# Attention and max-of-three kernel: ScalarE's background casts behind the copies of transposes, transposes ahead of the products where a group begins, and a tile order that alternates by heads

## The chip, the core and the metric

One NeuronCore of a Trainium2 chip runs the whole program. The metric is the device time of one execution in microseconds (us). A kernel's time is the median of its runs. The profile is of one execution, taken apart by engine: TensorE (PE, with its weight loads as PEld), VectorE (DVE), ScalarE (ACT), GpSimd (POOL), and SyncE (SP), whose queue issues almost all DMAs.

## What is computed

Attention with a relative-position bias that a small network makes, for 4 batches, 8 heads, 576 positions and 64 channels a head, and behind it a feed-forward stage with the greatest of three products:

```python
scores = scale * np.matmul(q, k.transpose(0, 1, 3, 2))
h = np.maximum(x @ w1 + b1, 0.0)          # x: relative log distances, 576 x 576
bias = h @ w2                             # 576 x 576 x 8 heads
scores = scores + bias.transpose(2, 0, 1)[None, :, :, :]
scores = scores - np.max(scores, axis=-1, keepdims=True)
attn = np.exp(scores)
attn = attn / (np.sum(attn, axis=-1, keepdims=True) + 1e-09)
out = np.matmul(attn, v)
...
x = out.transpose(0, 2, 1, 3).reshape(B * S, H * D)      # 2304 x 512
h = np.maximum(np.maximum(x @ w1, x @ w2), x @ w3)       # 2304 x 768
return h @ w_out                                         # 2304 x 512
```

## The kernel before

The program has three stages. The first (to about 60 us) makes the bias for all heads and writes it to DRAM (`bias_d`). The second is attention, to about 334 us. The third is the feed-forward stage (`moe`), to the end; it multiplies in blocks, with every fp32 operand as a sum of a high and a low part.

Attention runs over *units*. A unit is a pair of heads (`hp`, 4 of them) of one batch (`b`, 4 of them): 16 units, taken in 8 *pairs* of units, two pairs per head pair. The 576 query rows of a unit are four tiles of 128 rows and 64 left over; the two leftovers of a pair of units share a fifth tile, the mixed one (`MIX`). A pair of units therefore has nine tiles, in the order of `STEPS` (L180): four of the first unit (0, 1, 2, 3), the mixed one, four of the second unit (2, 3, 0, 1). 72 tiles make 72 steps; five more empty the pipeline (`LAG` = 5).

Step n (`step`, L367) does the following, engine by engine, in program order:

- `front` (L237): TensorE multiplies queries by keys for tile n, in three terms of high and low parts, into two PSUM tiles `s` (one a head).
- then products (`pv`, L347) that stand in the list `pvq`: exponentials by values. A *group* is the products of one unit for 256 query columns (group 0) or 320 (group 1, with the leftover); it has five pieces (`NTQ + 1`), four over key tiles `vt` and one over the leftover keys `vl`. One to three pieces run in a step, by the list in L381, so that a group begins in the steps n with n modulo 9 equal to 1, 3, 5 and 7 and ends in the step behind it.
- `shift` (L260) on VectorE: adds the bias tile `bias_t[t]` (names `bias_75` to `bias_79` for the tiles t = 0 to 4), scales, and finds the row's extreme. `expo` (L272) on ScalarE: the exponential `e` with its row sum `sm`, for both heads.
- `split_x` (L361) on VectorE: copies a group's results from PSUM to `xb`.
- background (`more`, L391): the generators `w0`, `ex` and `lx` convert the weights of the last stage and split x. Each `next` issues one instruction on ScalarE, VectorE or POOL.
- `load_bias` (L168): in the second half of a head pair's last pair, the bias tile just used is loaded anew for the next head pair, by SP's queue.
- `norm` (L284): 1/sum on VectorE, multiplied on POOL, for step n − 1.
- `prep` (L212): ScalarE casts k or q of a later unit to its high part (`kh`, `qh`, L220) and POOL subtracts for the low part (`kl`, `ql`, L223).
- `flip` (L299) for tile n − 5: TensorE transposes the normalized exponentials, eight blocks into two PSUM tiles `tp` (L316; two buffers, one a head) and one block `lp` for leftover keys (L320). ScalarE copies head 0's `tp` and `lp` to the tile `et` (L411), VectorE head 1's (L413). For the mixed tile each of these copies is two, one for each unit. `et` is what the products read.

Every engine takes its instructions in the order in which this code issues them. Line 409 to 413 of `step`, before:

```python
tp0, tp1, left = self.flip(f)
for x in tp0 + left:
    nc.scalar.copy(*x)
for x in tp1:
    nc.vector.tensor_copy(*x)
```

Of the kernel before, what the change touches and what calls it, by code (L numbers as in the profile page):

```python
# [19 lines left out]
def kernel(  # L20
# [12 lines left out]
    nc = tc.nc  # L33
# [146 lines left out]
    STEPS = [(0, 0), (0, 1), (0, 2), (0, 3), (2, NTQ), (1, 2), (1, 3), (1, 0), (1, 1)]  # L180
# [7 lines left out]
    GW = 128 * 2  # L188

    class Attention:  # L190
# [46 lines left out]
        def front(self, n):  # L237
            pair, y = fronts[n]
            which, t = STEPS[y]
# [20 lines left out]
        def shift(self, n, h):  # L260
            t = STEPS[fronts[n][1]][1]
# [37 lines left out]
        def flip(self, n):  # L299
            pair, y = sched[n]  # L300
            which, t = STEPS[y]
# [27 lines left out]
        def queue_pv(self, un, c0, w0, ea, el):  # L329
            hp, b = units[un]  # L330
            u = self.data[un]
            made = []

            def pair(c):
                def run():
                    if c == 0:
                        self.split_x()

                        if un == len(units) - 1 and not c0:
                            made.append(ps_s("pvlast")[:, 0, 0:w0])  # L340
                        else:
                            made.append(psums[-1].tile([128, w0], F32, tag="pv", bufs=1, name=f"pv{un}_{c0}"))
# [5 lines left out]
                    if c == NTQ:  # L348
                        col = (b % (B // 2)) * S + c0
                        slot = ((1, 0), (2, 3))[hp // 2][b // (B // 2)]  # L350
                        for x in range(NX):
                            lo, hi = max(col, TW * x), min(col + w0, TW * x + TW)
                            if lo < hi:
                                self.done.append((pv[:, lo - col:hi - col],
                                                  raws[x][slot][:, hp % 2, lo - TW * x:hi - TW * x]))
# [11 lines left out]
        def step(self, n, more=()):  # L367
            m, f = n - 1, n - LAG
            if n < NSTEP:
                pair, y = fronts[n]  # L370
                which, t = STEPS[y]
# [18 lines left out]
            last = None  # L390
            for w in more:  # L391
                if last != "scalar":
                    last = next(w, None)
            if n < NSTEP and units[2 * pair + 1][1] == border[-1] and which and units[2 * pair][0] + 1 < HP:
                load_bias(units[2 * pair][0] + 1, t)
            if 0 <= m < NSTEP:
                self.norm(m)
            if n < NSTEP:
                k = n - (NS * pair + 6)
# [8 lines left out]
            if back:  # L408
                tp0, tp1, left = self.flip(f)
                for x in tp0 + left:  # L410
                    nc.scalar.copy(*x)  # L411
                for x in tp1:
                    nc.vector.tensor_copy(*x)  # L413
                pair, y = sched[f]
                for at, un, g in ((1, 0, 0), (MIX, 0, 1), (6, 1, 1), (8, 1, 0)):
                    if y == at:
# [579 lines left out]
```

## Time and profile before

| what | value |
|---|---|
| median of 3 runs | 613.27 us |
| lowest, highest | 609.05, 617.02 us |
| the profiled execution | 615.38 us |
| its span on the core | 613.6 us |
| TensorE busy | 584.1 us, 95% |
| VectorE, ScalarE, POOL busy | 438.4, 341.5, 318.1 us |
| mean granted clock of TensorE in the profiled execution | 0.989 of full |

The span runs from the first to the last instruction that the profile shows; the execution's own time is 1.8 us longer. A busy share is of the whole span, over stages with different limits. Matmuls are pipelined, their ends in the profile are modelled, and durations of neighbours overlap; how long a block of matmuls holds TensorE is read from its start to the start of the next block. In a row of the timeline, the bracket gives the engine's idle time before the instruction and what ended it.

### The profile page before, as it was taken

The page shows a single profiled execution, that of the slowest core. Times are in us where ns is not written, and L with a number is a line of the kernel's source. Part 1 is how long each engine was busy: PE and PEld are TensorE (multiplying, and loading weights), DVE is VectorE, ACT ScalarE, POOL GpSimd, SP SyncE. Part 2 cuts the span into 40 slices and gives each one's busy share as a digit, 9 for nine tenths or more (in the row PEclk, how much of TensorE's full clock was granted, in tenths as well). Part 3 has the DMA queues.
Part 4 walks back from the last instruction along what each step waited for, and adds up shares of the span by engine and source line. Part 5 has one row for each costly group of instructions (what it writes and reads, how often), then busy time and mean ns, then how long its engine had stood idle before and what let it go on. Part 6 is the DMA issues. An engine that isn't in the chain of part 4 may idle for free.

```text
span 613.6 us, 12110 instructions
## 1 busy us (share of the span) xinstructions
PE 584.1 (95%) x4368; PEld 467.0 (76%) x4368; DVE 438.4 (71%) x907; ACT 341.5 (56%) x790; POOL 318.1 (52%) x312
## 2 busy tenths in 40 slices
PE   8999999999979989898999999999999999999997
PEld 4456656566656757566666999999999999988886
DVE  7995688587777868677865889997999756722211
ACT  7996877777786878578764662223132122332332
POOL 2775655648465565538462025668766874600000
PEclk9999999899999999799999999999999999999999
DMA  5998418440764429241000042242114211754541
GB/s 168 263 360 275 133 42 286 131 140 36 219 211 121 129 79 282 79 136 46 21 21 35 1 138 68 88 138 69 35 36 137 87 35 35 228 164 150 170 146 70
DMA packets 70380, 76.84 MB, mean 125 GB/s; under 512 B 22832, under 2 KB 50864, under 8 KB 70320
## 3 DMA queue, kind: packets, MB, share of 16 engines
q1 hardware_dynamic: 70176, 75.77, 39.4%
q8 instruction: 35, 0.57, 0.4%
q10 hardware_dynamic: 144, 0.29, 0.1%
q14 instruction: 25, 0.20, 0.1%
HBM read 49.69 MB, written 26.36 MB: 124 GB/s over the span
## 4 chain that ended last, share of the span: by engine, by line
PE 78%; ACT 10%; DVE 4%; issue 4%; DMA 3%; POOL 0%; ACTq 0%; DVEq 0%; SPq 0%
PE pv L347 12%; PE p L530 10%; PE p L529 10%; PE p L531 10%; PE tp L316 8%; PE s L256 7%; ACT e L278 5%; PE o L802 4%; PE o L805 4%; PE o L803 4%; PE bp L135 3%; PE s L249 2%; DMA bias<-bias_d 1%; PE c L529 1%; PE c L531 1%
## 5 line engine op out<-in xcount | busy, mean ns | idle before, releaser
L290 POOL TENSOR_SCALAR e<-e,rc 128x576 f32<-128x576 f32 x144 | 105.6, 746 | 103.0 <-DVE rc L287 63.9
L278 ACT ACTIVATE e<-sn,nm 128x576 f32<-128x576 f32 x144 | 110.7, 771 | 61.5 <-DVE nm L266 58.8
L266 DVE CUSTOM_DVE_ANT_0 sn<-s,bias 128x576 f32<-128x576 f32 x144 | 103.3, 755 | 33.3 <-PE s L256 19.4
L347 PE MATMUL pv<-et,vt 128*64 128x320 f32 (+1 forms) x496 | 81.5, 441 | 16.0 <-ACT et L411 15.8
L316 PEld LDWEIGHTS tp<-ident,e 128*128 128x128 f32 x576 | 62.1, 141 | 32.6 <-issue 25.0
L413 DVE COPY et<-tp 128x512 f32<-128x512 f32 (+1 forms) x80 | 49.7, 630 | 42.7 <-PE tp L316 42.7
L316 PE MATMUL tp<-ident,e 128*128 128x128 f32 x576 | 79.4, 281 | 0.3 <-DVE et L413 0.2
L347 PEld LDWEIGHTS pv<-et,vt 128*64 128x64 f32 x496 | 37.1, 141 | 41.1 <-ACT et L411 22.7
L558 ACT COPY m<-p 128x384 f32<-128x384 f32 x24 | 11.5, 480 | 93.9 <-PE p L531 58.0
L422 DVE TENSOR_TENSOR hl<-hin,hh 128x768 fp32r<-128x768 f32 x18 | 18.2, 1010 | 50.1 <-ACT hh L756 50.1
L256 PE MATMUL s<-kh,qh 64*128 64x288 f32 x256 | 49.6, 346 | 4.4 <-DVE nm L266 3.5
L566 POOL TENSOR_TENSOR q<-mp,m 128x768 f32<-128x768 f32 x18 | 33.8, 1880 | 36.2 <-DVE mp L422 36.2
L223 POOL TENSOR_TENSOR kl<-kr,kh 128x576 fp32r<-128x576 f32 x16 | 41.3, 2584 | 12.8 <-ACT kh L220 12.7
L411 ACT COPY et<-tp 128x512 f32<-128x512 f32 (+1 forms) x80 | 41.8, 533 | 8.8 <-PE tp L316 6.5
L422 DVE TENSOR_TENSOR ht<-ht,q 128x768 f32<-128x768 f32 x36 | 45.8, 1311 | 0.0
L422 POOL TENSOR_TENSOR wl<-wr,wh 128x256 fp32r<-128x256 f32 x25 | 23.6, 957 | 41.5 <-ACT wh L599 39.4
L802 PE MATMUL o<-woh,hh 128*128 128x512 f32 (+1 forms) x114 | 43.5, 385 | 0.0
L135 PE MATMUL bp<-hid,w2s 128*32 128x79 f32 (+51 forms) x640 | 41.0, 391 | 2.4 <-DVE hid L114 2.1
L803 PE MATMUL o<-wol,hh 128*128 128x512 f32 (+1 forms) x114 | 43.0, 381 | 0.0
L806 ACT COPY ot<-o 128x512 f32<-128x512 f32 (+1 forms) x19 | 10.7, 564 | 56.3 <-PE o L805 56.3
L256 PE MATMUL s<-kl,qh 64*128 64x288 f32 x256 | 41.7, 299 | 0.0
L256 PE MATMUL s<-kh,ql 64*128 64x288 f32 x256 | 40.6, 294 | 0.4 <-POOL ql L223 0.4
(175 smaller groups left out, 1491.4 us busy)
## 6 DMA issues: line engine op xcount, KB each, us to landing
bias_d<-bs SPq DMA_DIRECT2D x36, 295.5 KB, 5.6
bias<-bias_d SPq DMA_DIRECT2D x16, 576.0 KB, 5.7
w<-in_moe_w_dram SPq DMA_DIRECT2D x36, 256.0 KB, 3.4
h_d<-ht SPq DMA_DIRECT2D x18, 384.0 KB, 2.9
hin<-h_d SPq DMA_DIRECT2D x18, 384.0 KB, 3.9
qr<-in_qd_dram SPq DMA_DIRECT2D x16, 288.0 KB, 4.7
kr<-in_kd_dram SPq DMA_DIRECT2D x16, 288.0 KB, 4.7
out_dram<-ot SPq DMA_DIRECT2D x17, 256.0 KB, 4.0
```

Source lines behind the costliest of these rows:

```text
L256: nc.tensor.matmul(ss[h][:, x, 0:HALF], lhsT=u[q][p, 128 * t:128 * t + 128], rhs=u[k][p, cols], start=(j == 0), stop=(j == 2))
L266: nc.vector.tensor_tensor_reduce(out=sn.rearrange("p (a b) -> p a b", a=2), in0=st["s"][h][:, :, 0:HALF], in1=bt.rearrange("p (a b) -> p a ...
L278: nc.scalar.activation(st["e"][:, S * h:S * h + S], sn, ACTF.Exp, scale=-1.0, bias=nm, accum_out=st["sm"][:, h:h + 1])
L290: nc.gpsimd.tensor_scalar(out=e, in0=e, scalar1=rc[:, h:h + 1], scalar2=1.0, op0=ALU.mult, op1=ALU.mult)
L316: nc.tensor.transpose(tp[:, 128 * c:128 * c + 128], e2[:, k0:k0 + 128], ident)
L347: nc.tensor.matmul(pv[p], lhsT=w, rhs=x, start=(c == 0), stop=(c == NTQ))
L422: eng.tensor_tensor(out=out, in0=f(a), in1=f(b), op=op)
L529: nc.tensor.matmul(o, lhsT=hi[:, c], rhs=h[:, j], start=first and j == 0, stop=False)
L530: nc.tensor.matmul(o, lhsT=hi[:, c], rhs=l[:, j], start=False, stop=False)
L531: nc.tensor.matmul(o, lhsT=lo[:, c], rhs=h[:, j], start=False, stop=last and j == 1)
L802: nc.tensor.matmul(po, lhsT=hh[:, f], rhs=woh[:, r], start=(f == 0), stop=False)
L803: nc.tensor.matmul(po, lhsT=hh[:, f], rhs=wol[:, r], start=False, stop=False)
```

## The change

Three things change, all in attention.

1. *Tile order.* `STEPS` becomes two orders, `ORDERS`, chosen by `step_of` from the head pair: an even head pair keeps 0, 1, 2, 3, mixed, 2, 3, 0, 1; an odd one takes 2, 3, 0, 1, mixed, 0, 1, 2, 3. The second unit of a head pair's last pair thus ends its tiles in the order in which the next head pair begins them. A group's columns follow: group 0 of an odd head pair holds tiles 2 and 3, and group 1 tiles 0 and 1 with the leftover, whose columns lie apart. `queue_pv` therefore takes its results apart into `ranges`; `split_x` has 64 copies where it had 48.
2. *Transposes ahead of the products.* In the steps in which a group begins (n modulo 9 equal to 1, 3, 5, 7: `behind`), `flip` runs before the products. The copies stay where they were.
3. *ScalarE's order.* The copies of the transposes, leftovers in between, now stand before `prep` and before the background's ScalarE instructions. The background generators say before each instruction whether it is one for ScalarE (`"scalar"`) or another (`"vector"`), and the class `Stream` issues them in two calls: `go(False)` where the background stood, `go(True)` at the end of the step. How many are issued per step is set anew in the loop over n.

The core of the diff:

```diff
-    STEPS = [(0, 0), (0, 1), (0, 2), (0, 3), (2, NTQ), (1, 2), (1, 3), (1, 0), (1, 1)]
+    ORDERS = [[(0, x), (0, x + 1), (0, z), (0, z + 1), (2, NTQ), (1, z), (1, z + 1), (1, x), (1, x + 1)]
+              for x, z in ((0, 2), (2, 0))]
+    STEPS = ORDERS[0]
...
+    def step_of(pair, y):
+        return ORDERS[units[2 * pair][0] % 2][y]
...
-                    self.group(un, t // 2)
+                    self.group(un, int(y == 2))
...
-        def queue_pv(self, un, c0, w0, ea, el):
+        def queue_pv(self, un, g, ea, el):
...
+            x = GW if (hp + g) % 2 else 0
+            ranges = [(x, GW)] + ([(2 * GW, LEFT)] if g else [])
...
+            back = 0 <= f < NSTEP
+            behind = n % NS in (1, 3, 5, 7)
+            if behind and back:
+                flipped = self.flip(f)
             for _ in range((1, 3, 2, 3, 2, 3, 2, 2, 2)[n % NS]):
                 if self.pvq:
                     self.pvq.pop(0)()
-            back = 0 <= f < NSTEP
             if n < NSTEP:
                 for h in range(2):
                     self.shift(n, h)
                     self.expo(n, h)
             self.split_x()
-            last = None
             for w in more:
-                if last != "scalar":
-                    last = next(w, None)
+                w.go(False)
...
             if 0 <= m < NSTEP:
                 self.norm(m)
+            if back:
+                if not behind:
+                    flipped = self.flip(f)
+                tp0, tp1, left = flipped
+                for x, y in zip(tp0, left):
+                    nc.scalar.copy(*x)
+                    nc.scalar.copy(*y)
+                for x in tp1:
+                    nc.vector.tensor_copy(*x)
...
             if n < NSTEP:
+                pair, y = fronts[n]
                 k = n - (NS * pair + 6)
...
-            if back:
-                tp0, tp1, left = self.flip(f)
-                for x in tp0 + left:
-                    nc.scalar.copy(*x)
-                for x in tp1:
-                    nc.vector.tensor_copy(*x)
...
+            for w in dict.fromkeys(more):
+                w.go(True)
+
+    class Stream:
+        def __init__(self, gen):
+            self.gen = gen
+            self.next = next(gen, None)
+
+        def go(self, scalar):
+            if self.next == ("scalar" if scalar else "vector"):
+                self.next = next(self.gen, None)
...
-            more = [w0] if n >= NS - 1 else []
-            if n >= 36 and n % NS in (0, 4):
-                more.insert(0, ex)
-            if n >= NS - 1 and n % NS in (1, 3, 5, 8) and n < NSTEP:
-                more.append(w0)
-            if n >= NSTEP + 2:
-                more.insert(0, lx)
+            more = []
+            if n >= NS - 1 and n % NS:
+                more += [w0] * (2 if n % NS in (1, 3, 5) else 1)
+            if n >= 36 and n % NS in (2, 4, 6, 8):
+                more.append(ex)
+            if n >= NSTEP + 1:
+                more.append(lx)
```

ScalarE, step 45 (step 0 of the sixth pair, in which the mixed tile is flipped), before. `e` are the exponentials, `sm` their sum, `b11h`, `wao` and `kh` background casts, `et<-tp` and `et<-lp` the copies of the transposes:

```order
L278 ACTIVATE e_3347,sm_3348<-sn_0_3344,nm_0_3345 128x576
L278 ACTIVATE e_3347,sm_3348<-sn_1_3350,nm_1_3351 128x576
L282 ACTIVATE sm_3348<-sm_3348 128x2
L445 CAST b11h_3356<-xb_0_908 128x768
L470 ACTIVATE wao_3362<-w64o_3139 128x512
L220 CAST kh_3368<-kr_3102 128x576
L411 COPY et_1_3262<-tp_4_0_3373 128x4x64
L411 COPY et_1_3372<-tp_4_0_3373 128x4x64
L411 COPY et_1_3262<-lp_4_3383 128x64
L411 COPY et_1_3372<-lp_4_3383 128x64
```

The same step now:

```order
L285 ACTIVATE e_3370,sm_3371<-sn_0_3367,nm_0_3368 128x576
L285 ACTIVATE e_3370,sm_3371<-sn_1_3373,nm_1_3374 128x576
L289 ACTIVATE sm_3371<-sm_3371 128x2
L418 COPY et_1_3251<-tp_4_0_3384 128x4x64
L419 COPY et_1_3251<-lp_4_3394 128x64
L418 COPY et_1_3383<-tp_4_0_3384 128x4x64
L419 COPY et_1_3383<-lp_4_3394 128x64
L227 CAST kh_3402<-kr_3118 128x576
```

The copies moved from behind three casts to directly behind the sum; two of the casts moved to other steps, `kh` behind the copies.

TensorE, step 46 (step 1 of that pair), before: the end of its scores, the first six products of a group, the transposes, and the next step's scores:

```order
L256 MATMUL s_1_0_3391<-kh_3199,ql_3259 128x288
L256 MATMUL s_1_1_3392<-kh_3199,ql_3259 128x288
L347 MATMUL pv_256_3405<-et_1_3262,vt_2991 64x320 x6
L316 MATMUL tp_5_0_3433<-ident,e_3130 128x128 x4
L316 MATMUL tp_5_1_3438<-ident,e_3130 128x128 x4
L320 MATMUL lp_5_3443<-ident,e_3130 128x128
L256 MATMUL s_2_0_3448<-kh_3199,qh_3258 128x288
```

The same step now:

```order
L263 MATMUL s_1_0_3406<-kh_3228,ql_3294 128x288
L263 MATMUL s_1_1_3407<-kh_3228,ql_3294 128x288
L323 MATMUL tp_5_0_3420<-ident,e_3159 128x128 x4
L323 MATMUL tp_5_1_3425<-ident,e_3159 128x128 x4
L327 MATMUL lp_5_3430<-ident,e_3159 128x128
L358 MATMUL pv_1_3432<-et_1_3251,vt_2998 64x320 x6
L263 MATMUL s_2_0_3463<-kh_3228,qh_3293 128x288
```

The six products moved behind the nine transposes.

VectorE, the last step of the first head pair and the first of the second, before (`sn` is `shift`'s result; `bias_76` is tile 1, `bias_75` tile 0):

```order
L266 ISA sn_0_1772,nm_0_1773<-s_8_0_1754,bias_76 128x576
L266 ISA nm_0_1773 128x1
L266 ISA sn_1_1778,nm_1_1779<-s_8_1_1755,bias_76 128x576
L266 ISA nm_1_1779 128x1
L287 RECIPROCAL rc_1786<-sm_1719 128x2
L413 COPY et_1_1738<-tp_3_1_1795 128x4x128
L266 ISA sn_0_1821,nm_0_1822<-s_0_0_1805,bias_75 128x576
```

The same place now (`bias_77` is tile 2):

```order
L273 ISA sn_0_1773,nm_0_1774<-s_8_0_1755,bias_76 128x576
L273 ISA nm_0_1774 128x1
L273 ISA sn_1_1779,nm_1_1780<-s_8_1_1756,bias_76 128x576
L273 ISA nm_1_1780 128x1
L294 RECIPROCAL rc_1786<-sm_1733 128x2
L421 COPY et_1_1711<-tp_3_1_1795 128x4x128
L273 ISA sn_0_1821,nm_0_1822<-s_0_0_1805,bias_77 128x576
```

The first bias tile of the new head pair is tile 2 instead of tile 0; the loads stand in SP's queue in the order 2, 3, 0, 1 in both at this place.

## Rows read from the trace of the kernel before

**Rows 1.** The page: busy time by engine, and the chain that ended last.

```profile
PE 584.1 (95%) x4368; PEld 467.0 (76%) x4368; DVE 438.4 (71%) x907; ACT 341.5 (56%) x790; POOL 318.1 (52%) x312
...
PE 78%; ACT 10%; DVE 4%; issue 4%; DMA 3%; POOL 0%; ACTq 0%; DVEq 0%; SPq 0%
```

**Rows 2.** Busy time by stretch; columns in the first row.

```profile
core 0: us, PE busy (x) PEld busy (x) DVE busy (x) ACT busy (x) POOL busy (x), PEclk, DMA share, GB/s
334.00:613.60 279.60, 275.83 (x1494) 262.15 (x1494) 186.45 (x244) 86.65 (x145) 122.35 (x105) 1.00 0.32 100
...
252.40:256.10 3.70, 3.66 (x13) 2.10 (x14) 3.44 (x8) 2.61 (x9) 2.82 (x3) 0.50 0.01 2
...
217.40:219.30 1.90, 1.87 (x13) 0.88 (x14) 0.14 (x2) 1.90 (x7) 1.90 (x2) 1.00 0.00 0
```

**Rows 3.** Who waited for whom: us in total, times, longest.

```profile
PE pv L347 <- ACT et L411: 15.8, 17, 2.3
```

**Rows 4.** The chain in order of time, 126 to 131 us: start, us, what.

```profile
127.66 1.02 PE tp L316 x8
...
128.80 0.99 PE s L256 x12
```

**Rows 5.** Timeline, steps 6 and 7 of the fifth pair: start, us, engine, line.

```profile
201.88 0.65 PE L347 MATMUL pv<-et,vt 128*64 128x256 f32 x4
...
202.84 0.78 ACT L278 ACTIVATE e<-sn,nm 128x576 f32<-128x576 f32 x1 [0.55 <-DVE nm L266]
...
204.03 0.40 PE L256 MATMUL s<-kh,qh 64*128 64x288 f32 x2
...
204.61 0.66 ACT L220 CAST kh<-kr 128x576 fp32r<-128x576 f32 x1
...
205.17 0.58 ACT L411 COPY et<-tp 128x512 f32<-128x512 f32 x1
...
205.80 1.15 PE L347 MATMUL pv<-et,vt 128*64 128x256 f32 x8 [0.71 <-ACT et L411]
```

**Rows 6.** Timeline, steps 0 and 1 of the sixth pair.

```profile
212.73 1.09 PE L316 MATMUL tp<-ident,e 128*128 128x128 f32 x8
...
215.17 0.81 ACT L445 CAST b11h<-xb 128x768 fp32r<-128x768 f32 x1
...
217.43 1.84 PE L347 MATMUL pv<-et,vt 128*64 128x320 f32 x12 [2.34 <-ACT et L411]
```

**Rows 7.** Timeline, the third change of bias (steps 7, 0 and 1).

```profile
243.41 1.41 SPq L170 DMA_DIRECT2D bias<-bias_d  x2
...
246.61 1.09 PE L316 MATMUL tp<-ident,e 128*128 128x128 f32 x8
...
248.83 0.76 DVE L266 CUSTOM_DVE_ANT_0 sn<-s,bias 128x576 f32<-128x576 f32 x1 [2.94 <-DMA bias<-bias_d]
...
252.44 3.62 PE L347 MATMUL pv<-et,vt 128*64 128x320 f32 x12 [0.31 <-ACT et L411]
```

**Rows 8.** Timeline, the first change of bias (steps 0 and 1).

```profile
109.24 1.09 PE L316 MATMUL tp<-ident,e 128*128 128x128 f32 x8
...
113.38 3.39 PE L347 MATMUL pv<-et,vt 128*64 128x320 f32 x12 [1.05 <-ACT et L411]
```

**Rows 9.** Timeline, steps 0 and 1 of a pair without a change of bias.

```profile
143.60 0.65 PE L347 MATMUL pv<-et,vl 128*64 128x256 f32 x4
...
144.18 1.09 PE L316 MATMUL tp<-ident,e 128*128 128x128 f32 x8
...
147.21 0.64 ACT L411 COPY et<-tp 128x256 f32<-128x256 f32 x2
...
147.62 1.83 PE L347 MATMUL pv<-et,vt 128*64 128x320 f32 x12 [1.04 <-ACT et L411]
147.74 0.34 ACT L411 COPY et<-lp 128x64 f32<-128x64 f32 x2
```

**Rows 10.** Timeline of TensorE at the one place where scores waited for ql.

```profile
283.85 0.40 PE L256 MATMUL s<-kh,ql 64*128 64x288 f32 x2 [0.36 <-POOL ql L223]
```

**Rows 11.** The line L363, split_x's copies, by form: min/median/max ns.

```profile
L363 DVE COPY xb<-pv x46: 214/350/493, 77.3 to 329.1; 128x192 f32<-128x192 f32 x15, 128x256 f32<-128x256 f32 x8, 128x128 f32<-128x128 f32 x8, 128x320 f32<-128x320 f32 x8
```

More of the change, by code (lines that the diff above doesn't have):

```diff
@@ L238, in front @@
             pair, y = fronts[n]
-            which, t = STEPS[y]
+            which, t = step_of(pair, y)
             ss = [ps_s(f"s{pair}_{y}_{h}") for h in range(2)]
@@ L300, in flip @@
             pair, y = sched[n]
-            which, t = STEPS[y]
+            which, t = step_of(pair, y)
             pool, e2 = self.pool, self.st.pop(fronts.index((pair, y)))["e"]
@@ L332, in queue_pv @@
             made = []
+            x = GW if (hp + g) % 2 else 0
+            ranges = [(x, GW)] + ([(2 * GW, LEFT)] if g else [])
+            w0 = sum(w for _, w in ranges)
+            last = un == len(units) - 1 and not g
             def pair(c):
@@ L337, in run @@
                         self.split_x()
-                        if un == len(units) - 1 and not c0:
+                        if last:
                             made.append(ps_s("pvlast")[:, 0, 0:w0])
                         else:
-                            made.append(psums[-1].tile([128, w0], F32, tag="pv", bufs=1, name=f"pv{un}_{c0}"))
+                            made.append(psums[-1].tile([128, w0], F32, tag="pv", bufs=1, name=f"pv{un}_{g}"))
                     pv = made[0]
@@ L348, in run @@
                     if c == NTQ:
-                        col = (b % (B // 2)) * S + c0
                         slot = ((1, 0), (2, 3))[hp // 2][b // (B // 2)]
[L351 to L355, printed above, removed]
+                        o = 0
+                        for c0, w in ranges:
+                            col = (b % (B // 2)) * S + c0
+                            for x in range(NX):
+                                lo, hi = max(col, TW * x), min(col + w, TW * x + TW)
+                                if lo < hi:
+                                    self.done.append((pv[:, o + lo - col:o + hi - col],
+                                                      raws[x][slot][:, hp % 2, lo - TW * x:hi - TW * x]))
+                            o += w
                 return run
@@ L370, in step @@
                 pair, y = fronts[n]
-                which, t = STEPS[y]
+                which, t = step_of(pair, y)
                 un = 2 * pair + which
@@ L397, in step @@
                 self.norm(m)
+            if back:
[7 more added lines that the diff above has]
+                    nc.vector.tensor_copy(*x)
+                pair, y = sched[f]
+                for at, un, g in ((1, 0, 0), (MIX, 0, 1), (6, 1, 1), (8, 1, 0)):
+                    if y == at:
+                        self.queue_pv(2 * pair + un, g, *self.et[2 * pair + un])
             if n < NSTEP:
+                pair, y = fronts[n]
                 k = n - (NS * pair + 6)
@@ L407, in step, with rest @@
                     next(self.splits)
-            if back:
-                tp0, tp1, left = self.flip(f)
-                for x in tp0 + left:
-                    nc.scalar.copy(*x)
-                for x in tp1:
-                    nc.vector.tensor_copy(*x)
-                pair, y = sched[f]
-                for at, un, g in ((1, 0, 0), (MIX, 0, 1), (6, 1, 1), (8, 1, 0)):
-                    if y == at:
-                        self.queue_pv(2 * pair + un, GW * g, S - GW if g else GW, *self.et[2 * pair + un])
+            for w in dict.fromkeys(more):
[7 more added lines that the diff above has]
+                self.next = next(self.gen, None)
+        def rest(self):
+            while self.next:
+                self.next = next(self.gen, None)
     def arith(eng, out, a, b, op=ALU.subtract):
@@ L668, in begin @@
                     sumgen[s] = sum_w(*made_w[s])
+                    next(sumgen[s])
                 for k, y in enumerate((0, 1, 4, 5)):
@@ L671, in moe @@
                         at(n + 2, y, F(begin, s + 1))
-                    at(n + 2, y, lambda s=s: next(sumgen[s + 1]))
+                    at(n + 2, y, lambda s=s: next(sumgen[s + 1], None))
         sumgen = {}
@@ L691, in moe, with advance @@
         ww = work_w()
+        started = []
+        def advance():
+            if not started:
+                started.append(next(ww))
+            next(ww, None)
         at(2, 0, F(get, 4, 0))
@@ L892, in first @@
             last.update(raw=raw, sr=sr)
-        w0 = first()
+        w0 = Stream(first())
         x0 = Blocks(0, xa, xa)
@@ L935 @@
             at.pvq.pop(0)()
-        for w in (ex, lx, w0):
-            for k, _ in enumerate(w):
-                print("left over", w, k)
+        for w in (w0, ex, lx):
+            w.rest()
         x0.sum("t3")
```

54 lines of the change are left out of this document (25 added, 29 removed).

## The prediction

> **What bounds the kernel now.** I read the page first. TensorE is busy for 95% of the span and holds 78% of the chain that ended last; ScalarE holds 10% of that chain, VectorE 4% [rows 1]. An average over two stages hides where time can be won, so next came busy time by stretch: from 334 us to the end TensorE has work in 275.83 of 279.60 us, at a granted clock of 1.00 [rows 2]. The change touches nothing there. What it can win lies in the attention stage, 60 to 334 us.
>
> There I asked who waited for whom. TensorE's products waited 15.8 us, in 17 places, for ScalarE's copies of the transposes [rows 3]. Going through TensorE's timeline step by step shows that those places are regular. A pair of units is nine steps, numbered n modulo 9 here. In steps 0, 2, 3, 4, 5, 6, 8 TensorE is dense: 1.13 us of transposes, 0.99 of scores, then products [rows 4]. It stands still at two places of a pair.
>
> (a) Step 7, eight times. Scores start at 204.03, products at 205.80: 1.77 us where the scores need 0.99, so 0.78 us are lost. Meanwhile ScalarE ended its exponentials, cast kh (0.66 us) and only then copied the transposes [rows 5].
>
> (b) Step 1, seven times. From the start of step 0's transposes to the start of step 1's products 1.13 + 0.99 = 2.12 us would do. The undisturbed case takes 144.18 to 147.62 = 3.44, lost 1.32 [rows 9]; where three casts stand before the copies (the first of them in the rows), 212.73 to 217.43 = 4.70, lost 2.58 [rows 6]. The four cases without a bias change lose 1.57, 1.32, 2.58 and 1.01 (the two others are read alike): 6.5 us.
>
> (c) The three steps 1 that follow a change of bias take 4.14 [rows 8], 5.15 and 5.83 us [rows 7], lost 2.02 + 3.03 + 3.71 = 8.8. The last shows why: the load of bias tile 0 is issued at 243.41, two steps before its use, and VectorE waits 2.94 us for it. Behind each of the three the twelve products take 3.39, 3.39 and 3.62 us instead of 1.84 [rows 6 to 8], because the granted clock there is 0.50, the 1.2 GHz level [rows 2]: 1.55 + 1.55 + 1.78 = 4.9 us more. So (c) costs 13.7.
>
> **The change, part by part.** *Tile order by heads.* A bias tile is reloaded once its last use in a head pair is over. Before, tile 0 is free in step 7 of one pair and needed in step 0 of the next; now the tile freed in step 5 is the first one needed, so every tile has four steps instead of two; nine steps made 34.9 us (109.24 to 144.18) [rows 8, 9], so two are 7.8. VectorE's wait was 2.94 at most [rows 7], so it goes. What is late next in these three places is the ordinary wait (b). If the low clock follows that wait, it goes too: after the ordinary waits, up to 2.34 us long, the clock stood at 1.00 [rows 2, 6].
>
> The Trainium skill's page "TensorE: Matmul & The Clock Gate" (section "Why this matters for your kernels") advises against idle gaps between bursts of matmuls, since the clock falls back in them. By that rule the three slow stretches go with the waits and the sum is the one below; if they had another cause it would be 4.9 us smaller. The trace agrees in three places out of three, but the gap before 217.43 brought no fall.
>
> The order also splits products' results at other columns: VectorE has 16 more copies, of some 0.35 us or less [rows 11], 5.6 us at most over eight pairs. VectorE is busy 71% [rows 1] and these copies stand behind the work that TensorE waits for; I take 0, with 0 to 5.6 as ends.
>
> *Casts behind the copies.* No instruction is added to ScalarE; the order of the copies and casts of a step changes. In step 6 the 0.66 us cast goes from before to behind the copy. What is then left of (a)? Exponentials start 0.96 us after the scores' end (201.88 to 202.84), last 1.77 with the sum (to 204.61), and the copy 0.58 [rows 5]: 3.31 us after the scores' end. TensorE meanwhile has products and transposes (201.88 to 204.03 = 2.15) and the next scores, 0.99: 3.14. So about 0.2 us stay of 0.78.
>
> *Products behind the transposes in steps 1, 3, 5, 7.* The transposes now come first, and they wait too: their two PSUM buffers are those that the copies of the step before must have emptied. Products no longer wait, since 1.13 us of transposes lie ahead of them. So the wait passes from products to transposes, for the first half of the copies only.
>
> For step 1 this means: step 0 flips the mixed tile, whose copies are four: 0.64 for two halves and 0.34 for two leftovers [rows 9], now in the order half, leftover, half, leftover. The first transposes need both halves: 0.96 + 1.77 + 0.64 + 0.17 = 3.54 us after the scores' end. TensorE has products 0.58 (143.60 to 144.18) [rows 9], transposes 1.13 and scores 0.99 = 2.70. About 0.85 us stay, in each of the seven places. Bounds: nothing stays if VectorE starts its part sooner; 1.3, the ordinary wait of before, stays if the order gives nothing.
>
> *Background moved.* What a cast feeds comes later by the copies that it now follows, 0.85 us (0.58 and 0.27). POOL's ql follows the cast of qh, and scores waited for ql once, 0.36 us [rows 10]. Bounds: 0, or 0.85 in seven pairs = 6.0; I take 1.0, near the row. The order of loads in SP's queue is as before except which background load falls where, so I charge nothing.
>
> **Sum against the profiled execution.**
> (c) 13.7 − 3 × 0.85 = 11.1 won.
> (b) 6.5 − 4 × 0.85 = 3.1; one of these steps now has a late cast ahead of it, so 2.5.
> (a) 8 × (0.78 − 0.2) = 4.6.
> Two more waits for copies, of 0.71 and 0.21, are among the 17: 0.9.
> Late casts: −1.0.
> Together 18.1; I say 18. The profiled execution took 615.4, so 597.4 for it. It lies 2.1 us above the median of the runs, 613.27; from the median 18 less is 595.3.
> The ends: if every wait named goes and nothing comes back, 13.7 + 6.5 + 6.2 + 0.9 = 27 and 586. If step 1 keeps 1.3 seven times (−3.2), step 7 keeps all (−4.6) and casts cost 6 (−5), 5 are won and the time is 608; all at once is unlikely, so the forecast's own range is 588 to 601.
>
> **Rivals.**
> *The wait only changes hands.* Transposes stand where products stood and wait as long: the order of TensorE gives nothing and copies end as late as before because exponentials do. Then only (c) is won, less three ordinary waits: 13.7 − 3 × 1.32 = 9.7, so 603.5. For it: the same copies release both. Against it: rows 5 and 6 show one to three casts between exponentials and copies, and these go.
>
> *The low clock has another cause.* (c) loses 4.9 of its gain: 600.2. For it: the 2.34 us wait brought no fall. Against: all three falls stand behind a late bias and none elsewhere in the pairs.
>
> *The loads come no sooner.* SP's queue holds them up behind other loads as before, and VectorE still waits. Then 11.1 falls away: 606. Against it: they were late by 2.94 at most, and two steps are gained.
>
> *Slower: ScalarE becomes the bound.* Casts behind the copies stand in front of the next step's exponentials. ScalarE idled 0.55 us there [rows 5], a cast lasts 0.66. If the room shrinks to nothing because TensorE no longer stops, every cast delays exponentials by 0.66, these the copies, and these the transposes of the next step 1, 3, 5 or 7: 4 × 8 × 0.66 = 21 us, with (a) and (b) not won: 613.3 + 21 − 11 = 623. It decides as soon as ScalarE's work in a step with a cast is longer than TensorE's step in most steps; by rows 5 it is 0.1 us longer in a short step, and the next step without a cast makes that up. The Trainium skill's page "PSUM — Partial Sum Buffer" (section "Engine vs sequencer instructions") says that ScalarE takes its queue strictly in order and that matmuls start in program order: by that neither exponentials nor ready products can pass, so this rival has no way out once it begins. The trace agrees as far as it goes: the copies behind three casts waited for all of them.
>
> **How the numbers follow.** Forecast 0.72; wait changes hands 0.13; other cause of the clock 0.07; loads no sooner 0.04; slower 0.04. The line of 2%, about what a measurement of this kernel can tell from no change, is 601.0 us below and 625.5 above. Faster by more: the forecast and half of the clock's case, which lies near the line, 0.76. Slower by more: 0.03, part of the last rival. Within 2%: 0.21. Predicted 595.3; the range 588 to 605 takes in the changing of hands.
>
> **What would show it.** Right: no wait of VectorE for the bias; the products' 15.8 us for copies nearly gone, and in their place transposes waiting some 0.85 us in step 1 and 0.2 in step 7; all products of 12 near 1.84 us; the last stage as long as now, only sooner. Wrong: transposes that wait over 1.3 us, or scores that wait for ql or for VectorE in many pairs (ScalarE late), or a clock of 0.50 inside the stage.

## The result, and the profile after

The changed kernel takes 594.62 us (median of 4 runs, 593.48 to 597.03), the kernel before in the same comparison 615.14 us (4 runs, 609.05 to 618.24, the three shown earlier among them). The ratio is 0.970, with a 95% interval of 0.962 to 0.979: faster, and 0.7 us from the 595.3 us predicted. The profiled execution took 595.08 us, with a span of 592.2 us. Why the sum came out so close is another question: two of its terms were wrong, in opposite directions.

The page after, to be read beside [rows 1]:

```profile
PE 577.1 (97%) x4368; PEld 458.9 (77%) x4368; DVE 441.1 (74%) x923; ACT 340.6 (58%) x790; POOL 318.5 (54%) x312
...
PE 75%; ACT 9%; DVE 6%; DMA 4%; issue 4%; POOL 1%; SPq 0%; DVEq 0%; ACTq 0%; POOLq 0%
```

TensorE's busy time fell by 7.0 us with the same 4368 instructions, for the greater part the products that ran at the 1.2 GHz level in [rows 7, 8]. The rest is idle time that is gone. Busy time by stretch says where (columns as in [rows 2]):

```profile
62.00:312.60 250.60, 243.64 (x2122) 163.30 (x2120) 203.51 (x544) 202.24 (x552) 162.08 (x187) 1.00 0.42 129
312.60:592.20 279.60, 275.84 (x1494) 261.98 (x1494) 186.24 (x244) 86.77 (x145) 122.35 (x105) 1.00 0.31 100
```

The last stage is as long as before, 279.6 us; its first product starts at 312.7 instead of 334.2, 21.5 us sooner, and the granted clock of attention is 1.00. Who waits for whom, against the 15.8 us of [rows 3] (us in total, times, longest):

```profile
PEld tp L323 <- ACT et L418: 3.9, 14, 0.4
...
PE tp L323 <- ACT et L418: 1.9, 8, 0.2
...
PE s L263 <- POOL ql L230: 1.3, 2, 0.9
```

Products wait for no copy any more, VectorE waits for no bias, and every run of twelve products on 320 columns takes 1.78 to 1.84 us. What is left stands in three places. In step 7 the transposes wait for ScalarE's copy, now ahead of the cast (the same step as in [rows 5]):

```profile
194.28 0.57 ACT L418 COPY et<-tp 128x512 f32<-128x512 f32 x1
194.74 0.27 ACT L419 COPY et<-lp 128x128 f32<-128x128 f32 x1
194.90 0.68 ACT L227 CAST kh<-kr 128x576 fp32r<-128x576 f32 x1
194.99 1.07 PE L323 MATMUL tp<-ident,e 128*128 128x128 f32 x8 [0.25 <-ACT et L418]
```

From the scores' start (193.69) to the transposes are 1.30 us where 0.99 would do: 0.31 lost, in six of the eight pairs; 0.78 were lost before. The first pair loses 0.36 inside its transposes, where head 1's wait for POOL, and one pair loses nothing.

In step 1 of the same pair (to be read beside [rows 6, 9]):

```profile
171.71 0.40 PE L263 MATMUL s<-kh,qh 64*128 64x288 f32 x2
171.87 0.73 DVE L421 COPY et<-tp 128x256 f32<-128x256 f32 x2
...
172.73 0.35 ACT L418 COPY et<-tp 128x256 f32<-128x256 f32 x1
172.75 1.43 PE L323 MATMUL tp<-ident,e 128*128 128x128 f32 x8
172.98 0.21 ACT L419 COPY et<-lp 128x64 f32<-128x64 f32 x1
173.09 0.39 ACT L418 COPY et<-tp 128x256 f32<-128x256 f32 x1
...
173.52 0.42 PEld L323 LDWEIGHTS tp<-ident,e 128*128 128x128 f32 x4 [0.39 <-ACT et L418]
...
174.22 1.83 PE L358 MATMUL pv<-et,vt 128*64 128x320 f32 x12
```

The eight transposes begin at 172.75, before ScalarE's copies are done, because head 0's four go into the buffer that VectorE emptied at 172.60. Only head 1's four wait, until ScalarE's third copy ends at 173.48. Scores to scores, step 1 takes 4.28 us here (171.71 to 175.99) where 3.89 would do (0.99 of scores, 1.13 of transposes, 1.77 of products): 0.4 lost. Over seven pairs it is 3.9 us. Of these 1.15 stand in the sixth pair, and some 0.7 of them are no wait for copies: the scores themselves wait for VectorE there.

```profile
204.32 0.40 PE L263 MATMUL s<-kh,qh 64*128 64x288 f32 x1 [0.26 <-DVE nm L273]
```

Third, the scores of step 0 wait for ql in five pairs, 2.65 us in all: 1.2, 0.18, 0.65, 0.30 and 0.32.

### The profile page after: what moved, and what is told of

It is laid out like the page before. It is cut to its first block, busy times and chain, and to the rows that moved or that the text cites. A ratio compares the mean times of both kernels' runs of the same rounds, so it can differ in the third digit from the quotient of the medians.

```text
span 592.2 us, 12085 instructions
## 1 busy us (share of the span) xinstructions
PE 577.1 (97%) x4368; PEld 458.9 (77%) x4368; DVE 441.1 (74%) x923; ACT 340.6 (58%) x790; POOL 318.5 (54%) x312
## 4 chain that ended last, share of the span: by engine, by line
PE 75%; ACT 9%; DVE 6%; DMA 4%; issue 4%; POOL 1%; SPq 0%; DVEq 0%; ACTq 0%; POOLq 0%
PE pv L358 10%; PE p L564 10%; PE p L565 10%; PE p L566 10%; PE tp L323 7%; PE s L263 6%; ACT e L285 4%; PE o L845 4%; PE o L848 4%; PE o L846 4%; PE bp L135 3%; DMA kr<-in_kd_dram 2%; DVE sn L273 2%; PE c L564 1%; ACT et L418 1%
## 5 line engine op out<-in xcount | busy, mean ns | idle before, releaser
L273 DVE CUSTOM_DVE_ANT_0 sn<-s,bias 128x576 f32<-128x576 f32 x144 | 103.2, 753 | 41.9 <-PE s L263 31.2
L358 PE MATMUL pv<-et,vt 128*64 128x320 f32 (+1 forms) x496 | 73.6, 419 | 0.0
L601 POOL TENSOR_TENSOR q<-mp,m 128x768 f32<-128x768 f32 x18 | 33.9, 1881 | 36.0 <-DVE mp L457 36.0
L230 POOL TENSOR_TENSOR kl<-kr,kh 128x576 fp32r<-128x576 f32 x16 | 42.5, 2658 | 18.4 <-ACT kh L227 18.2
L358 PEld LDWEIGHTS pv<-et,vt 128*64 128x64 f32 x496 | 30.2, 136 | 24.8 <-issue 11.4
L263 PE MATMUL s<-kh,qh 64*128 64x288 f32 x256 | 47.8, 344 | 1.4 <-ACT bs L155 0.9
L263 PEld LDWEIGHTS s<-kh,qh 64*128 64x128 f32 x256 | 26.3, 184 | 18.8 <-issue 8.9
```

Of the source, the lines that this page charges most:

```text
L263: nc.tensor.matmul(ss[h][:, x, 0:HALF], lhsT=u[q][p, 128 * t:128 * t + 128], rhs=u[k][p, cols], start=(j == 0), stop=(j == 2))
L273: nc.vector.tensor_tensor_reduce(out=sn.rearrange("p (a b) -> p a b", a=2), in0=st["s"][h][:, :, 0:HALF], in1=bt.rearrange("p (a b) -> p a ...
L358: nc.tensor.matmul(pv[p], lhsT=w, rhs=x, start=(c == 0), stop=(c == NTQ))
```

## The experiments

The three edits can each be undone alone or made alone, which gives all eight combinations. One thing was never undone: how many background instructions fall in which step. This new distribution stands in all kernels below, and only the kernel before lacks it. The combinations come first, then what tests the two buffers, then two edits that go further. Each kernel was compared with the kernel before on the same chip; that one's medians there were 613.87 (one edit undone, and head 0 from ScalarE), 614.06 (one edit alone, and head 0 from VectorE) and 612.92 us (the last three). The changed kernel was not run again in these comparisons, so a difference from its 594.62 us is one between comparisons, and where it is small the traces have to show it.

**Tile order undone.**

```diff
-              for x, z in ((0, 2), (2, 0))]
+              for x, z in ((0, 2), (0, 2))]
...
-            x = GW if (hp + g) % 2 else 0
+            x = GW if g else 0
```

> The changed kernel, but with the tile order the same for all head pairs, as before (the order of ScalarE's work and of products and transposes stays changed). Main theory (the tile order buys the early bias tile and with it the clock, 10 to 11 us): VectorE waits for the bias again at the three bias changes, 2 to 3 us each, three stretches at a granted clock of 0.50 come back with products of twelve at 3.4 to 3.6 us, and the time is 604 to 608. Rival (the low clock had another cause, the copies' wait or the products' place): the bias waits return but the products of twelve stay at 1.84 and the time is 599 to 602. Rival (the other two edits do the whole): 594 to 597.

Measured: 603.18 us (601.39 to 604.46), 8.6 us more than the changed kernel; a little under the main theory's range. The waits for the bias return (who waits for whom):

```profile
DVE sn L273 <- DMA bias<-bias_d: 8.1, 3, 4.3
PE s L263 <- DVE nm L273: 5.7, 8, 1.9
```

But the clock fell behind two of the three, not all. TensorE's scores at the three changes (timeline):

```profile
112.30 0.39 PE L263 MATMUL s<-kh,qh 64*128 64x288 f32 x1 [1.88 <-DVE nm L273]
...
178.04 0.39 PE L263 MATMUL s<-kh,qh 64*128 64x288 f32 x1 [1.40 <-DVE nm L273]
...
243.66 0.40 PE L263 MATMUL s<-kh,qh 64*128 64x288 f32 x1 [1.09 <-DVE nm L273]
```

By stretch, the first change of bias and the second (columns as in [rows 2]):

```profile
112.00:114.00 2.00, 1.41 (x11) 1.20 (x12) 2.00 (x9) 1.63 (x4) 0.43 (x1) 0.81 0.03 9
114.00:116.00 2.00, 2.00 (x12) 1.72 (x9) 1.57 (x6) 2.00 (x7) 1.41 (x3) 0.50 0.00 0
...
178.00:180.00 2.00, 1.51 (x13) 1.10 (x14) 2.00 (x8) 1.89 (x6) 0.70 (x1) 1.00 0.00 0
180.00:182.00 2.00, 1.92 (x15) 1.26 (x17) 1.97 (x6) 2.00 (x8) 1.42 (x3) 1.00 0.04 8
```

Behind the third, the mean clock was 0.59 from 246 to 248 us and 0.56 from 248 to 250. The shortest of the three waits was followed by a fall and a longer one was not, so the length of the wait alone does not decide.

**Products ahead of transposes again.**

```diff
-            behind = n % NS in (1, 3, 5, 7)
+            behind = False
```

> The changed kernel, but products stand ahead of transposes in every step, as before. Main theory (products behind transposes only shortens the wait by the second half of the copies, since the products need all four copies of the mixed tile and the transposes only the first half): products wait about 0.9 us in step 1 instead of the transposes' 0.4, seven times, step 7 as now, so 3 to 4 us more: 597 to 599. Rival (the order of TensorE gives nothing): 594 to 596. Rival (it gives the whole gain of steps 1 and 7): 602 to 605.

Measured: 595.25 us (594.94 to 596.39). The rival is right: beside the other two edits, TensorE's order is worth 0.6 us in the medians, inside the spread of the changed kernel's runs. The timeline of step 1 shows where my theory went wrong:

```profile
172.86 0.29 PE L263 MATMUL s<-kh,ql 64*128 64x288 f32 x2
...
173.12 0.35 ACT L418 COPY et<-tp 128x256 f32<-128x256 f32 x1
...
173.52 1.83 PE L358 MATMUL pv<-et,vt 128*64 128x320 f32 x12 [0.37 <-ACT et L418]
```

The first products need only the first of ScalarE's four copies (173.12 to 173.47), the half of the unit whose group begins. Transposes of head 1 need the third as well. So products ahead wait 0.36 to 0.48 us in step 1, and transposes ahead 0.4: the same.

**ScalarE's order undone.** The casts (`prep`) and the background go back ahead of the copies; halves and leftovers stay in turn.

```diff
             if 0 <= m < NSTEP:
                 self.norm(m)
+            for w in dict.fromkeys(more):
+                w.go(True)
+            if n < NSTEP:
...
+                    next(self.splits)
             if back:
...
-            for w in dict.fromkeys(more):
-                w.go(True)
```

> The changed kernel, but ScalarE's casts and background work stand ahead of the copies of transposes in a step, as before. Main theory: the 0.66 us cast of kh in step 6 holds up the copies again, 0.4 to 0.7 us in each of eight steps 7, and one to three casts hold up those of step 0, 0.3 to 1.5 us in seven steps 1; transposes wait for copies some 8 to 10 us in all instead of 5.8; scores no longer wait for ql (1 to 2 us won back). Time 599 to 604. Rival (with the transposes first the casts are hidden): 594 to 596.

Measured: 602.60 us (602.39 to 604.06), as expected: 8.0 us more. What an order of ScalarE's queue can cost shows at one place, where the load of kr is late (timeline, step 6 and 7 of the second pair):

```profile
100.89 0.63 PE L323 MATMUL tp<-ident,e 128*128 128x128 f32 x4
102.33 0.67 ACT L227 CAST kh<-kr 128x576 fp32r<-128x576 f32 x1 [1.91 <-DMA kr<-in_kd_dram]
102.91 0.58 ACT L431 COPY et<-tp 128x512 f32<-128x512 f32 x1
...
103.64 0.63 PE L323 MATMUL tp<-ident,e 128*128 128x128 f32 x4 [2.12 <-ACT et L431]
```

The copy had its data, but stood behind a cast that waited 1.91 us for a DMA, and TensorE waited 2.12. The Trainium skill's page "PSUM — Partial Sum Buffer" (section "Engine vs sequencer instructions") says that ScalarE's queue is strictly first in, first out; the trace agrees. In the changed kernel the same load is 1.74 us late, the copies are through, and only the scores pay, for ql.

**One edit alone.** Each of these is the changed kernel with the other two undone, by the diffs above.

> The kernel before with the tile order by heads alone: ScalarE's casts and background ahead of the copies, products ahead of transposes. By my sum for the bias changes (13.7 us less three ordinary waits of 0.85) 11 us are won: 602 to 604. By what undoing the tile order cost in the changed kernel (8.6 us) it would be 605 to 606. Rival (the wait for the bias only hides the wait for copies, which then shows): 608 to 611. No wait for the bias and products of twelve at 1.84 us in all cases.

> The kernel before with ScalarE's order alone: copies ahead of casts and background, products ahead of transposes, the same tile order for all heads. If the order of TensorE is worth nothing, as the kernel with products ahead again showed (0.6 us), this is the kernel with the tile order undone: 603 to 605. Rival (with late bias tiles the order of TensorE does matter): 607 to 610. Waits for the bias of 1 to 4 us at three places, and the granted clock of 0.50 behind two or three of them.

> The kernel before with the order of TensorE alone: transposes ahead of products in steps 1, 3, 5 and 7, casts ahead of copies, the same tile order for all heads. If that order is worth nothing: 612 to 615. Rival (with casts in front of the copies the transposes do go ahead of a wait, since head 0's buffer is emptied by VectorE): 608 to 611, the products' wait for copies (15.8 us) replaced by a smaller one of the transposes.

All eight together (medians in us; waits in us from the profiles, those of TensorE's matmuls; with transposes first, some of the wait of step 1 stands inside a group of eight matmuls and shows only at their weight loads: 8.7, 8.6, 3.7 and 3.9 us in the four rows with transposes first; the first row also lacks the new distribution of the background):

| tile order | ScalarE's order | TensorE's order | median, range | mean clock of the runs | TensorE waits for ScalarE's copies | VectorE waits for the bias at a change |
|---|---|---|---|---|---|---|
| before | before | before | 614.06, 610.37 to 621.17 (16 runs) | 0.983 to 0.997 | 15.8 | 5.9 |
| by heads | before | before | 608.37, 607.28 to 609.48 | 0.996 to 1.000 | 18.7 | 0 |
| before | copies first | before | 605.14, 603.38 to 609.35 | 0.989 to 0.997 | 4.2 | 7.7 |
| before | before | transposes first | 610.38, 605.94 to 613.33 | 0.992 to 0.997 | 9.4 | 2.3 |
| by heads | copies first | before | 595.25, 594.94 to 596.39 | 0.999 to 1.000 | 4.0 | 0 |
| by heads | before | transposes first | 602.60, 602.39 to 604.06 | 0.997 to 1.000 | 9.2 | 0 |
| before | copies first | transposes first | 603.18, 601.39 to 604.46 | 0.993 to 0.997 | 1.8 | 8.1 |
| by heads | copies first | transposes first | 594.62, 593.48 to 597.03 | 0.999 to 1.000 | 1.9 | 0 |

Four things can be read from it. First, the tile order. Against the kernel before it is worth 5.7 us, less than any figure I gave but that of its own rival, and the waits for copies are 18.7 us instead of 15.8:

```profile
PE pv L358 <- ACT et L431: 18.7, 19, 2.0
```

But they did not take the place of the wait for the bias. From the scores of step 0 to the end of step 1, the three changes of bias took 33.9 us before and take 22.8 with this edit alone, 11.1 less; and the waits for copies in the seven steps 1 fell, from 9.0 to 6.6 us. They grew in steps 7 (6.0 to 8.1), 3 (0.2 to 2.0) and 5 (0.7 to 1.9). About 1.3 us of that is a load of kr that came later. Most of the rest stands behind background casts that the new distribution puts into these steps, here still ahead of the copies (timeline, step 7 of the fourth pair; before, `kh` stood there alone and products waited 0.75):

```profile
169.29 0.66 ACT L506 ACTIVATE wao<-w64o 128x512 f32<-128x512 f32 x1
169.85 0.66 ACT L227 CAST kh<-kr 128x576 fp32r<-128x576 f32 x1
170.42 0.58 ACT L431 COPY et<-tp 128x512 f32<-128x512 f32 x1
...
171.04 1.15 PE L358 MATMUL pv<-et,vt 128*64 128x256 f32 x8 [1.28 <-ACT et L431]
```

Second, ScalarE's order. Against the kernel before it is worth 8.9 us. The wait for the bias grew there, from 5.9 to 7.7 us in all, and at the first change from 1.42 to 4.00: TensorE gets there sooner, and VectorE can start with the bias no sooner (110.38 against 109.77).

Together the two give 18.8 us, 4.2 more than the two alone. That is no proof that one hides the other's gain, since each gain against the kernel before holds the new distribution as well. A kernel with that distribution and all three edits undone was not run. Rows that share the distribution and differ in one edit give 7.8, 8.6 and 9.9 us for the tile order, whatever else is there, and 13.1, 8.0 and 7.2 us for ScalarE's order.

Third, TensorE's order is a substitute for ScalarE's. With the tile order it gives 5.8 us, since it cuts the waits for copies (18.7 to 9.2); behind ScalarE's order 0.6 to 2.0 remain. Where it stands, ScalarE's order is worth 8.0 instead of 13.1. Alone, against the kernel before, it gives 3.7.

The fourth reading is the clock. The kernel before ran between 610.37 us at a mean clock of 0.997 and 619.23 at 0.989 (the slowest of its 16 runs, 621.17 at 0.983, left out), and in another comparison once at 1.000, in 608.78 us. The other kernels with the old tile order lay between 0.989 and 0.997, those with the new one between 0.996 and 1.000. The profiled execution of before was one draw from that spread. The fall is not bound to the bias either. In the profile of the tile order alone VectorE waits for no bias, and yet one stretch of attention is at 0.50, behind a late load of kr (timeline, and by stretch with columns as in [rows 2]):

```profile
102.56 0.67 ACT L227 CAST kh<-kr 128x576 fp32r<-128x576 f32 x1 [1.20 <-DMA kr<-in_kd_dram]
...
103.76 1.15 PE L358 MATMUL pv<-et,vt 128*64 128x256 f32 x8 [2.01 <-ACT et L431]
```

```profile
104.80:108.20 3.40, 3.40 (x21) 3.02 (x21) 0.69 (x1) 2.11 (x6) 3.40 (x5) 0.50 1.15 342
```

With TensorE's order alone the same load and a wait of 1.67 us had 0.50 behind them too. With ScalarE's order undone TensorE waited 2.12 us for it, and the clock stayed at 1.00.

**Head 0's buffer always from ScalarE.**

```diff
-        return psums[-1].tile([128, 512], F32, tag="t", bufs=2, name=name)
+        return psums[-1].tile([128, 512], F32, tag=f"t{x}", bufs=1, name=name)
...
-                tp = ps_t(f"tp{pair}_{y}_{h}")
+                tp = ps_t(f"tp{pair}_{y}_{h}", h)
```

> The changed kernel, but each head's transposes have a PSUM buffer of their own, so head 0's always take the one that ScalarE emptied, and head 1's the one that VectorE emptied. In the changed kernel the two buffers change hands, and in six of the seven steps 1 head 0 takes VectorE's. Theory (that is why the step 1 lost 0.4 us and not the 0.85 that I worked out): head 0's transposes now wait in step 1 as well, step 1 loses 0.8 to 0.9 us in each of the six, 2.5 to 3 us more in all: 596.5 to 598.5; step 7 as now. Rival (the smaller loss comes from copies that are themselves sooner, whoever empties the buffer): step 1 loses 0.4 to 0.5 as now, 594 to 595.5.

Measured: 598.54 us (598.46 to 598.60), 3.9 more. The theory holds, and its size is a little over the range. Step 1 of the same pair as above (timeline):

```profile
174.44 0.39 ACT L418 COPY et<-tp 128x256 f32<-128x256 f32 x1
...
174.88 1.09 PE L323 MATMUL tp<-ident,e 128*128 128x128 f32 x8 [0.76 <-ACT et L418]
```

All eight transposes now wait, 0.76 to 0.88 us in each of the seven steps 1. That is the 0.85 of my prediction: it was right for a kernel in which head 0 takes ScalarE's buffer. By the traces the seven steps 1 take 3.05 us more together, as the theory had it; another 1.1 stands in one step 3.

**Head 0's buffer always from VectorE.** The same with `(h + n) % 2` in the place of `h`.

> The changed kernel, but the two PSUM buffers of transposes change hands in every step, so that head 0's transposes always take the one that VectorE emptied. Theory (step 7 keeps 0.31 us because there head 0 takes ScalarE's buffer in seven of eight pairs; the one pair where it takes VectorE's keeps nothing): the seven waits of 0.24 go and 7 x 0.31 = 2.2 us are won: 592 to 593. Rival (head 1 then waits as long, or VectorE's copy is no sooner): 594 to 595.

Measured: 595.12 us (594.62 to 595.49). The rival is right. In step 7 VectorE's copy is no sooner than ScalarE's (timeline, the same step as above):

```profile
194.44 0.67 DVE L421 COPY et<-tp 128x512 f32<-128x512 f32 x1
194.46 0.57 ACT L418 COPY et<-tp 128x512 f32<-128x512 f32 x1
...
195.25 1.06 PE L323 MATMUL tp<-ident,e 128*128 128x128 f32 x8 [0.33 <-DVE et L421]
```

VectorE did 0.92 us of background ahead of it, and its copy ended at 195.11, ScalarE's at 195.03. That VectorE frees its buffer first holds in step 1, not in general: here two of the eight steps 7 lose nothing, where one did in the changed kernel.

**Step 1 split.** Head 0's transposes, then products, then head 1's transposes.

```diff
+                if between and h == 0:
+                    between()
...
+            inside = behind and back and n % NS == 1
             if behind and back:
-                flipped = self.flip(f)
+                flipped = self.flip(f, products if inside else None)
```

> The changed kernel, but in step 1 TensorE does head 0's transposes, then the products, then head 1's transposes. Theory: the first product needs only the first of ScalarE's four copies, and head 1's transposes need the third; with head 0's 0.5 us of transposes ahead the products wait for nothing, and 1.8 us of products cover the copies that head 1 needs. The 0.4 us that step 1 loses go in the five or six pairs where head 0 takes VectorE's buffer: 2.0 to 2.5 us won, 592 to 593. Rival (VectorE's copies of head 1 come 1.8 us later and hold up head 0 of step 2): 594 to 597.

Measured: 593.98 us (592.68 to 594.91). No wait shows in the step 1 that was shown above: scores to scores it takes 4.06 us (172.21 to 176.27) instead of 4.28. The seven steps 1 take 29.9 us together instead of 31.2, so the trace shows 1.3 won. The median is 0.6 us lower, within the spread of either kernel, so the gain of 2 us is not shown; neither is the rival's loss.

**ql early.** In step 7 the cast of qh goes ahead of the copies and ql ahead of POOL's normalization.

```diff
+            soon = n < NSTEP and n % NS == 7
+            if soon and 2 * fronts[n][0] + 2 < len(units):
+                next(self.splits)
             if 0 <= m < NSTEP:
                 self.norm(m)
...
-                if 0 <= k < 2 and 2 * pair + 2 < len(units):
+                if k == 0 and 2 * pair + 2 < len(units):
```

> The changed kernel, but the cast of qh in step 7 stands ahead of that step's copies, and ql ahead of the normalization of e on POOL. Theory: ql is ready 0.7 to 1.4 us sooner, the scores of step 0 no longer wait for it (2.65 us lost over five pairs, some 2 of them won), and the copies of step 7, 0.7 us later, are still ahead of step 8's transposes, which stand behind products: 592 to 593.5. Rival (step 8's transposes or e come late instead): 594.5 to 599.

Measured: 592.33 us (590.88 to 593.70), 2.3 us less, as the theory had it. The ranges of the two kernels overlap a little and the comparisons differ, so the traces decide: the seven steps 0 take 19.0 us together instead of 21.7, none of them over 2.76. In the changed kernel ql ended at 201.10 and the scores waited 0.38 us for it; here it ends at 200.87, before they begin (timeline, steps 7 to 0):

```profile
198.70 0.66 ACT L227 CAST qh<-qr 128x576 fp32r<-128x576 f32 x1
...
199.44 1.43 POOL L230 TENSOR_TENSOR ql<-qr,qh 128x576 fp32r<-128x576 f32 x1 [0.84 <-ACT qh L227]
200.84 2.43 POOL L297 TENSOR_SCALAR e<-e,rc 128x576 f32<-128x576 f32 x2
...
201.39 0.40 PE L263 MATMUL s<-kh,qh 64*128 64x288 f32 x2
```

POOL idles 0.84 us for the cast and normalizes later; nobody waits for that here, since the transposes read it four steps later.

**Both.**

> The two edits of the kernels before this in the list together: step 1 split, and ql early. If both theories hold, their gains add: 590 to 591.5. If neither does: 594.5 or more.

Measured: 591.18 us (590.43 to 591.50), ratio to before 0.9665 (0.963 to 0.970). All its runs lie under the fastest of the changed kernel (593.48). It beats both kernels, by 3.4 us in the medians against the changed one; the two were timed in different comparisons. Its steps 0 and 1 take 2.7 and 1.7 us less than in the changed kernel, so the two gains do add.

## Why the prediction was right

**The bias and the clock (c), 11.1 us: right.** The wait for the bias goes, the clock stays at 1.00 and the products of twelve are at 1.84 us, as the text had it. The three places, from the scores of step 0 to the end of step 1, take 22.9 us instead of 33.9: 11.1 won, though two differences met in it. They keep 0.4, 0.4 and 0.6 us at step 1 instead of 0.85 each, and pay 1.7 for late ql, which the prediction charged apart. Undoing the tile order costs 8.6 us in the medians; in that kernel's profile the clock fell behind two changes instead of three. The old profile's 4.9 us for the clock were one execution's share: in the runs it comes and goes.

**Casts behind the copies, (a) and (b), 4.6 + 2.5 + 0.9: right.** Together 8.0, or 7.0 with the late casts taken off. Undoing ScalarE's order costs 8.0, but partly in other places than reckoned, since the background's new distribution stays: 4.8 us in the steps 7, 2.9 in the steps 1, 2.6 in the steps 3 and 5, less 1.9 in the steps 0, where ql is in time again. From before to after, the steps 7 gain 5.1 us (4.6 were reckoned), and the four other pairs of steps 0 and 1 gain 3.6, with 1.0 of late ql already off (2.5 were reckoned). Step 7 keeps 0.31 us in six pairs and 0.36 in one instead of 0.2 in eight, 2.2 against 1.6.

**Products behind the transposes, 0.85 us left in step 1: wrong in two steps of the working.** "The first transposes need both halves" holds for one head only: 0.4 were left, as head 0 took VectorE's buffer; with ScalarE's buffer forced on it, 0.76 to 0.88 were. And I took it that products ahead would wait longer, when they need only the first copy. The seven places keep 3.9 us where 7 × 0.85 + 0.6 = 6.6 were reckoned. What the text gave to TensorE's order as such is worth 0.6 us in the medians once ScalarE's copies come first.

**Late casts, 1.0 us: mis-sized.** They cost 2.65. The bound (0 to 6.0) held, and the value near the row was too low, because ql stands behind POOL's normalization as well as behind the cast: in the fifth pair ScalarE ends the cast of qh at 198.86, POOL normalizes from 198.25 and begins ql at 199.68. Part of it, 1.2 us, is a load of kr that came 1.74 us late; I had charged nothing for the loads.

**Why the sum held.** What I left to remain was 1.6 + 6.6 + 1.0 = 9.2 us, and what remained is 2.2 + 3.9 + 2.65 = 8.75. The 2.7 us too many at step 1 met 0.6 and 1.65 too few elsewhere. The profiled executions differ by 20.3 us, the medians by 18.7 (from 613.27) and 20.5 (from 615.14), against 18. That the median lies within 0.7 us is luck in part: errors of 1.65 and 2.7 us cancelled, and the kernel before's own median moved between 612.92 and 615.14 from one comparison to the next.

**The rivals.** The wait only changes hands: refuted, by 594.62 us against its 603.5; but its remark that the order of TensorE gives nothing is nearly right (0.6 us). The low clock has another cause: not for the three stretches of before, which went with the late bias; but a late load of kr brought the fall too, in two kernels that have the casts ahead of the copies, and not each late load did. The loads come no sooner: no. ScalarE becomes the bound: no, TensorE is busy 97%. But one sign that the prediction named for being wrong did come: scores waited for ql in five of the seven steps 0.

## What to carry to other kernels

On an engine that takes its queue in order, work that nobody waits for belongs behind the copies that free a buffer, and a cast whose load may be late belongs behind them all the more. An edit's worth depends on what else is in the kernel: ScalarE's order gave 13.1 us without TensorE's and 8.0 with it, so try each from the start and undo each from the end. List every part of a change, too: the background's new distribution stayed in each of these kernels, and against the one kernel that lacks it the tile order looked worth 5.7 us instead of 7.8 to 9.9. Before charging a wait for a buffer, look up which engine emptied that very buffer, and which of several copies the first reader needs.

## What the runs showed of the hardware

The Trainium skill's page "TensorE: Matmul & The Clock Gate" (section "Why this matters for your kernels") advises against idle gaps between bursts of matmuls, and means gaps longer than any wait of TensorE told of here. So that section did not say by itself that the three slow stretches would go. The runs agree in direction: in the changed kernel and the one with products ahead the mean clock is 0.999 or more, and the spread of the runs is 3.6 and 1.5 us (four runs each) against 8.9 for before (15 runs, its slowest left out; more runs also spread wider). In all the profiles, the stretches at 0.50 inside attention stand behind a late load, of the bias or of kr; that shorter gaps can bring the fall is what these runs add. They don't show what decides one case: waits of TensorE of 2.01, 1.88 and 1.09 us were followed by a fall, and others of 2.12 and 1.40 us, and in the kernel before one of 2.34 us [rows 2, 6], by a clock of 1.00. That was not settled here.
